# Gated mix of two long convolutions: B's results multiplied by u on the way out of PSUM, mix summing in TensorE, a new fixed order

## The chip, the cores and the metric

One core of a Trainium2 chip runs the whole kernel. The metric is the time of one execution in microseconds (us) on the device; of several executions the median counts. The engines are TensorE (PE in the profile, with its weight loads as PEld), VectorE (DVE), ScalarE (ACT), GpSimd (POOL) and SyncE (SP, which here only issues DMAs). PSUM is the memory that TensorE writes its results to, SBUF the working memory.

## The reference

Two sequence convolutions over 2048 positions and 448 channels, both with the same input u, are mixed by a gate:

```
x = A_u
g = sigmoid((x * gate_w).sum(-1, keepdims=True))
a = A(x)      # S4: x convolved with K[d,l] = Re sum_n C B dt exp(dt A l), N = 256 modes, plus x * Dskip
b = B(x)      # H3: kv = shift(k) * v; y = kv convolved with ssm_k, plus kv * ssm_D; b = x * y
out = g * a + (1 - g) * b
```

So B's convolution y is multiplied by x, element by element, before it is mixed. All inputs and the output are bf16. Written with a - b, the mix is out = b + g * (a - b), and this is how the kernel computes it.

## The kernel before

**Layout.** The 448 channels are handled as 4 groups g of 112, which lie beside one another on the partitions; each group's 112 are cut into four quarters H of NC = 28. All work runs quarter by quarter. `natu` holds u and `natv` holds kv, later B's results, each as 128 partitions x 64 x 112; `ug[H]` is the window of one quarter in `natv`, `uu` is u in `natu`. A quarter of either is 128x1792.

**Stages.** `PLAN` (line 37) gives the order in which they are written down: T0 B0 T1 b1 a0 T2 b2 a1 T3 b3 a2 m0 m1 m2 A3. T is `table(H)` (1032), which makes S4's kernel K for a quarter: exponentials and sines on ACT, products into the tiles TP and TQ on DVE, some sums by DMA with an add, and then TensorE. B and b are `conv_B(H)`, A and a are `conv_A(H)` (1055), m is `mix(H)` (1071). A convolution is a two-stage transform of both operands by matrices on TensorE (`spread`, then `transform`, 407), whose results DVE or ACT copies out of PSUM; `swapped` (803) exchanges the two halves of the partitions of one operand in eight DMAs; `products` (478) multiplies on DVE, 128x3584 twice; then come the two stages back, `stage_a` (438) and stage B. Stage B multiplies with the weights G. A b and an a that follow one another share it: `stage_b_both` (448) computes sixteen rows of B's quarter and of A's quarter in one PSUM room. In the same room TensorE subtracts B's finished results from A's with the weights `minus` (a negative identity matrix), so the room holds y of the one and a - b of another quarter's.

**What is done with the results.** For A, `epilogue_A` multiplies by the gate on the way out of PSUM (`gated`, 973) and writes over u in `natu`, since that quarter's u is no longer needed. For B, `epilogue_B` (948) copies PSUM into `ug[H]`, and after the last part of a quarter DVE multiplies the whole quarter by u. `mix(H)` adds `ug[H]` (b) and the window of `natu` (g * (a - b)) on DVE and carries the sum to the output's layout with `relay` (965): for each of the four groups four matmuls with 32 columns of `minus` each, which run side by side in the four column groups of TensorE. Their result has the wrong sign, and the copy out of PSUM (`evac.minus`) turns it. The last quarter, A3, goes through `end` (980) instead, which does the same in four parts.

**Who does what, and when.** Nothing of this is left to a scheduler. Four strings fix it, and each is indexed by the running number of a call: `SLOTS` says which of eight SBUF buffers a stage takes (the tiles q of the profile), `ROOMS` which of four PSUM rooms (the tiles ps), each 2 x 512 f32 per partition, `SIDES` which engine does each copy out of PSUM and each small scaling (S is ScalarE, V is VectorE), and for each half-tile swap which queue issues it (V is GpSimd's, S is SyncE's). All instructions are recorded as calls, and `ORDER` lists their numbers; `issue` of the class `Order` (133) issues them in this order and ties each to the one before it on its engine. So an engine runs its instructions strictly in the written order, and an instruction that waits holds up all behind it on its engine. Since every call goes through the same line of `issue`, all instructions carry line 145 in the profile; what tells them apart is tile, shape and time.

**Setup.** `Modes.run` (718) takes S4's coefficients from PSUM into the tiles hold. `hold` is a list of three tiles of one, one and two quarters; for each there are two copies for each of two coefficients.

Of the kernel before, what the change touches and what calls it, by code (L numbers as in the profile page):

```python
# [10 lines left out]
ALU = mybir.AluOpType  # L11
# [13 lines left out]
NC = 112 // NQG  # L25
# [6 lines left out]
HALVES = 1  # L32
Q_ROWS = {0: 0, 256: 1, 4: 2, 260: 3, 2: 4, 512: 5, 6: 6, 768: 7, 1024: 8, 1280: 9, 1536: 10,
# [5 lines left out]
    "60254113451327565066707216435622473722641555230367571061240"  # L39
)  # L40
ROOMS = (
    "303201320132221133023000100332000020101102013331223132233010132231223133020313021221212111021000320232120101311331120231"
    "31230230312202203230211002013123100022133320222302200321202302202333012331301212103331312131332201202032310"
)
SIDES = (
    "SSSSVVSVVVVSVVSVVVVVVVVVSVVVSSVVVSSSSSVSVVSSVVSVVSVSSVVSVVVVVVVSSSSSSSSSSSSSSSSSVVVSVSSSVSSSSSSSSSSSSSSSSVSSSSVSVSSSSSSS"
    "SSSSSSSSSSSSSVSSVSSSSSSSSSSVSSSSSSSSSSSSSSSSSSVVSVSSSSSSSSSSSSSSSSSVVVVVVVVVSVVSVVVSSSSSSVSSSSSSSSSSSSVVSVSSSSSSSSSSVSVV"
    "SSSSSSSSSSSVSSSVVSSSSSSSSSSSVSSSSVVVVVVVVSVVVVSVVVSSSVSVVSSSSSSSSSSVVVSVVSSSSSSSSSSSSSSVSSSSSVSSSSSSVSSVSVSSVSSSSVSVVSSS"
    "VSSSSVSSVVVVSSSSSSSSSSVVVSSSSVSSSSVSSSVVSS"
)  # L50
ORDER = (
# [520 lines left out]
class Part:  # L572
# [71 lines left out]
    def tables(self, H, E):  # L644
# [20 lines left out]
        add(TQ, 4, 25, 2, 2)  # L665
        q(15, 2, 2, -2, 256)
# [78 lines left out]
def body(  # L745
# [381 lines left out]
```

## Time and profile before

| | |
|---|---|
| median of three runs | 249.86 us (248.34 to 250.38) |
| the profiled execution, its own time | 247.59 us |
| its span, from first to last instruction | 245.7 us |
| mean granted clock of TensorE | 0.984 of full speed |

| stretch of the span | PE busy | DVE busy | ACT busy |
|---|---|---|---|
| 0 to 60 us | 41.1 | 57.3 | 52.4 |
| 60 to 203 us | 133.5 | 139.2 | 142.1 |
| 203 to 237 us | 33.4 | 32.7 | 23.9 |
| 237 to 245.7 us | 1.3 | 2.2 | 0.5 |

A busy time is the sum of an engine's instruction durations, with the overlap of neighbours taken out. PE's ends are modelled, so a PE that is busy all the time may still have room. A group of instructions in the profile reads: line, engine, operation, written tile <- read tiles, shapes and types, number; then busy time in us, the mean duration of one in ns; then the idle time of the engine just before them and what ended it. The chain of waits is the way back from the last instruction, at each step to what released it. The profile is that of one execution, so terms of a sum that come from it are to be set beside 247.59, not beside the median.

### The profile page before, as it was taken

To read this page: it belongs to the slowest core of one execution; us is meant where nothing else is said; L and a number is where in the kernel's file an instruction comes from. 1 tells how busy PE (TensorE), PEld (TensorE's weight loads), DVE (VectorE), ACT (ScalarE), POOL (GpSimd) and SP (SyncE) were. 2 spreads that over 40 slices of the span, in tenths; PEclk is the share of its full clock that TensorE was granted. 3 is DMA by queue.
4 is the path that set the end of the run, shared out by engine and by line. 5 is a ranking of instruction groups with operands and counts; after the bars stand their busy time and mean duration, and the time that the engine had idled before them with its cause. 6 is when DMAs were issued, how large, how long until landed. Compare 5 with 4: busy or idle time off the path is not lost.

```text
span 245.7 us, 12199 instructions
## 1 busy us (share of the span) xinstructions
PE 209.4 (85%) x5451; PEld 185.2 (75%) x5451; DVE 231.3 (94%) x399; ACT 219.0 (89%) x335; POOL 37.5 (15%) x109
## 2 busy tenths in 40 slices
PE   1557688888989999888999977999999999999970
PEld 1445256766979899788998866889999998998850
DVE  6999999999888999999999999999999999999980
ACT  3897999989999999999999999999999998657820
POOL 8600003040000014000002320000134220300000
PEclk9999799999999999999999999999999999999996
DMA  6999599999002189300476593000248720230046
GB/s 140 311 191 147 123 190 229 188 204 167 7 5 64 39 197 205 93 4 5 78 114 122 104 226 100 7 3 5 39 80 152 187 80 5 63 95 3 3 105 197
DMA packets 43443, 26.27 MB, mean 107 GB/s; under 512 B 34144, under 2 KB 40400, under 8 KB 43392
## 3 DMA queue, kind: packets, MB, share of 16 engines
q1 hardware_dynamic: 39088, 15.98, 30.6%
q0 software_dynamic: 3456, 8.60, 17.6%
q10 hardware_dynamic: 848, 0.92, 1.3%
q8 instruction: 42, 0.69, 1.1%
q14 instruction: 9, 0.07, 0.1%
HBM read 9.78 MB, written 2.87 MB: 51 GB/s over the span
## 4 chain that ended last, share of the span: by engine, by line
DVE 34%; ACT 32%; PE 21%; issue 6%; DMA 5%; DVEq 0%; ACTq 0%
PE ps L145 21%; ACT q L145 21%; DVE TQ L145 10%; DVE TP L145 9%; DVE q L145 6%; ACT G L145 4%; DVE natv L145 3%; DMA TP<-TP 2%; ACT ET L145 2%; ACT s_W L145 1%; DMA RK<-in_A_log_dt_dram 1%; DVE RK L145 1%; ACT RK L145 1%; DMA out_dram<-q 1%; DVE ET L145 1%
## 5 line engine op out<-in xcount | busy, mean ns | idle before, releaser
L145 ACT CAST q<-ps 128x896 bf16<-128x896 f32 (+3 forms) x168 | 131.6, 909 | 6.6 <-PE ps L145 6.4
L145 PEld LDWEIGHTS <-G 128*128 128x128 bf16 (+2 forms) x1136 | 35.5, 103 | 15.0 <-issue 6.0
L145 DVE TENSOR_TENSOR TQ<-TQ,ET 128x896 bf16<-128x896 bf16 (+2 forms) x70 | 45.9, 683 | 0.1
L145 PEld LDWEIGHTS <-q 128*128 128x128 bf16 (+2 forms) x784 | 41.0, 134 | 6.3 <-issue 3.5
L145 PE MATMUL ps<-q,s_W 128*128 128x112 bf16 (+1 forms) x544 | 32.6, 210 | 4.5 <-ACT q L145 2.3
L145 PE MATMUL ps<-TP,TQ 128*32 128x32 bf16 x1792 | 32.7, 240 | 2.8 <-DVE TQ L145 1.7
L145 PE MATMUL ps<-sa_R,q 128*128 128x128 bf16 x448 | 33.0, 229 | 1.5 <-issue 1.0
L145 DVE TENSOR_TENSOR q<-q,q 128x3584 bf16<-128x3584 bf16 (+1 forms) x22 | 32.3, 1510 | 1.2 <-ACT q L145 0.9
L145 PEld LDWEIGHTS <-s_W 128*128 128x128 bf16 x544 | 27.6, 97 | 7.6 <-issue 5.5
L145 PEld LDWEIGHTS <-TQ 128*32 128x32 bf16 x1792 | 29.6, 153 | 4.9 <-DVE TQ L145 1.9
L145 DVE TENSOR_TENSOR TP<-TP,ET 128x1792 bf16<-128x1792 bf16 (+3 forms) x25 | 31.7, 1270 | 0.6 <-DMA TP<-TP 0.5
L145 ACT ACTIVATE q<-hold 128x224 bf16<-128x224 f32 (+1 forms) x77 | 28.8, 461 | 0.4 <-DVE hold L145 0.3
L145 POOL DMA_DIRECT2D TP<-TP x15 | 13.4, 958 | 102.3 <-DVE TP L145 33.5
L145 POOL DMA_DIRECT2D q<-q x27 | 15.8, 638 | 57.5 <-DVE q L145 24.4
L145 PEld LDWEIGHTS <-natu 128*64 128x64 bf16 (+1 forms) x288 | 21.0, 208 | 4.6 <-DMA natu<-in_B_k_dram 3.1
L145 PE MATMUL ps<-q,G 128*128 128x56 bf16 (+1 forms) x640 | 20.3, 182 | 0.2 <-ACT q L145 0.2
L145 ACT ACTIVATE ET<-q 128x1344 bf16<-128x1344 int16 (+1 forms) x12 | 17.2, 1456 | 1.1 <-DVE TQ L145 1.0
L145 PE MATMUL ps<-Wc,natu 128*64 128x128 bf16 x224 | 16.0, 285 | 0.2 <-ACT q L145 0.2
L145 PE MATMUL ps<-Wc,natv 128*64 128x128 bf16 x224 | 15.2, 283 | 0.4
L145 PEld LDWEIGHTS <-natv 128*64 128x64 bf16 x224 | 14.7, 212 | 1.1 <-issue 0.2
L145 DVE TENSOR_TENSOR TQ<-TQ 128x448 bf16<-128x448 bf16 (+2 forms) x35 | 15.3, 443 | 0.1
L145 PE MATMUL ps<-G 112*32 112x336 bf16 (+3 forms) x448 | 13.8, 274 | 1.3 <-DVE natv L145 1.1
(97 smaller groups left out, 289.6 us busy)
## 6 DMA issues: line engine op xcount, KB each, us to landing
q<-q SPq DMA_DIRECT2D x37, 112.0 KB, 3.7
TP<-TP POOLq DMA_DIRECT2D x9, 448.0 KB, 5.8
q<-q POOLq DMA_DIRECT2D x27, 112.0 KB, 3.9
natu<-in_B_k_dram SPq DMA_DIRECT2D x2, 896.0 KB, 7.2
natv<-in_B_v_dram SPq DMA_DIRECT2D x8, 224.0 KB, 4.7
q<-in_B_ssm_k_dram SPq DMA_DIRECT2D x16, 112.0 KB, 3.9
natu<-in_A_u_dram SPq DMA_DIRECT2D x8, 224.0 KB, 5.8
TP<-TP POOLq DMA_DIRECT2D x6, 224.0 KB, 4.0
```

Source lines behind the costliest of these rows:

```text
L145: ins = f(*args, **kw)
```

## The change

1. `epilogue_B` no longer copies. DVE reads B's results from PSUM, multiplies them by u and writes b into `ug[H]`, part by part: twelve instructions of 128x448 and two of 128x896. The fourteen copies (twelve on ACT, two on DVE) and the four multiplies of a whole quarter are gone.
2. `mix` has no add. Each relay is two matmuls into the same place of PSUM, the first with b, the second with g * (a - b), which accumulate: 96 where there were 48.
3. `Modes.run` takes both halves of a tile of one quarter out of PSUM in one copy: four copies of 128x224 in place of eight of 128x112.
4. `SLOTS`, `ROOMS`, `SIDES` and `ORDER` are new throughout. By the count of the instructions, DVE has 387 where it had 399 and ACT 337 where it had 335; ten of the 64 half-tile swaps move from SyncE's queue to GpSimd's (27 to 37).
5. A function `splits` and a tuple `LATE` are added. `LATE` is empty for every quarter, so none of it is issued.

```diff
+LATE = ((), (), (), ())
...
 SLOTS = (
-    "60254113451327565066707216435622473722641555230367571061240"
+    "73475502153230513610646232057112416355041222567603341505721"
 )
 ROOMS = (
...
 SIDES = (
...
 ORDER = (
...
+    def splits(self, dst, base, src, n, step, e):
...
-            q(25, 0, 2, 2, 2)
+        late = LATE[H]
+        if 4 in late:
+            self.splits((4, 6), 25, 0, 2, 2, 2)
+        else:
+            q(25, 0, 2, 2, 2)
...
             for h0, h1, t in self.hold:
+                src = pt[:, :, 0:448].rearrange("p f (g h w) -> p f g h w", g=4, w=NC)
+                if h1 - h0 == 1:
+                    evac(t[:, 0, c].rearrange("p (f g w) -> p f g w", f=2, w=NC), src[:, :, :, h0])
+                    continue
                 for f in range(2):
-                    evac(t[:, :, c].rearrange("p h (q w) -> p q h w", w=NC)[:, 4 * f:4 * f + 4],
-                         pt[:, f, 0:448].rearrange("p (g h w) -> p g h w", g=4, w=NC)[:, :, h0:h1])
+                    evac(t[:, :, c].rearrange("p h (q w) -> p q h w", w=NC)[:, 4 * f:4 * f + 4], src[:, f, :, h0:h1])
...
     def epilogue_B(H):
         def consume(b0, n, pt):
-            evac(banked(ug[H][:, b0:b0 + n], pt), pt)
-            if b0 + n == 64:
-                V.tensor_tensor(out=ug[H], in0=ug[H], in1=window(uu, 0, 64, H), op=ALU.mult)
+            V.tensor_tensor(out=banked(ug[H][:, b0:b0 + n], pt), in0=pt, in1=banked(window(uu, b0, n, H), pt), op=ALU.mult)
         return consume
...
     def mix(H):
-        o, x = ug[H], window(uu, 0, 64, H)
-        V.tensor_tensor(out=o, in0=o, in1=x, op=ALU.add)
+        a, b = window(uu, 0, 64, H), ug[H]
         for g0 in (0, 2):
             pt = places.room()
             for i in range(2):
-                relay(pt[:, i, 0:448], g0 + i, lambda x: o[:, 16 * x:16 * x + 16], True, True)
+                for j, t in enumerate((b, a)):
+                    relay(pt[:, i, 0:448], g0 + i, lambda x: t[:, 16 * x:16 * x + 16], j == 0, j == 1)
```

More of the change, by code (lines that the diff above doesn't have):

```diff
@@ L621, in add @@
                                      in0=half(0), in1=half(1), op=ALU.add)
+    def splits(self, dst, base, src, n, step, e):
+        m, T = self.m, self.TQ
+        r = self.ET[:, ENTRY[e], 1]
+        part = list(r.ap[0])
+        for i0 in range(0, n, n if dst[-1] - dst[0] == n - 1 else 1):
+            k = n if dst[-1] - dst[0] == n - 1 else 1
+            o, s = T[:, dst[i0]], T[:, src + i0 * step]
+            self.nc.vector.tensor_tensor(
+                out=bass.AP(o.tensor, o.offset, [list(o.ap[0]), [2 * m, k], [m, 2], [(base + i0 - dst[i0]) * 2 * m, 2], [1, m]]),
+                in0=bass.AP(s.tensor, s.offset, [list(s.ap[0]), [step * 2 * m, k], [0, 2], [m, 2], [1, m]]),
+                in1=bass.AP(r.tensor, r.offset, [part, [0, k], [-m, 2], [m, 2], [1, m]]), op=ALU.mult)
+        d = T[:, dst[0]]
+        to = bass.AP(d.tensor, d.offset, [list(d.ap[0]), [2 * m * (dst[-1] - dst[0]) // max(n - 1, 1), n], [1, 2 * m]])
+        self.nc.gpsimd.dma_start(out=to, in_=T[:, base:base + n].rearrange("p n c m -> p n (c m)"), accum_op=ALU.add)
     def pairs(self, base, src, n, step, e):
@@ L671, in tables @@
         add(TQ, 7, 27, 2, -2)
-        q(27, 5, 2, 2, 512)
-        self.back(8, 16)
-        add(TQ, 8, 27, 2)
+        if 8 in late:
+            self.splits((8, 9), 27, 5, 2, 2, 512)
+            self.back(8, 16)
+        else:
+            q(27, 5, 2, 2, 512)
+            self.back(8, 16)
+            add(TQ, 8, 27, 2)
         self.back(0, 8, E[:, 8:16])
-        q(29, 8, 1, 1, 512)
+        if 10 in late:
+            self.splits((10,), 29, 8, 1, 1, 512)
+        else:
+            q(29, 8, 1, 1, 512)
         pairs(27, 9, 1, 1, 512)
-        add(TQ, 10, 29, 1)
+        if 10 not in late:
+            add(TQ, 10, 29, 1)
         pairs(11, 6, 2, -2, 256)
```

15 lines of the change are left out of this document (8 added, 7 removed), and 119 rows, old and new, of the table ORDER.

## The prediction

> **What bounds the kernel now.** I read the page's totals first, then busy time by stretch, then the chain that ended last, and only then the groups of instructions that the change touches.
>
> ```profile
> span 245.7 us, 12199 instructions
> ...
> PE 209.4 (85%) x5451; PEld 185.2 (75%) x5451; DVE 231.3 (94%) x399; ACT 219.0 (89%) x335; POOL 37.5 (15%) x109
> ...
> DVE 34%; ACT 32%; PE 21%; issue 6%; DMA 5%; DVEq 0%; ACTq 0%
> ```
>
> DVE is idle for 14.4 us of the span (245.7 - 231.3), ACT for 26.7. The chain is shared between three engines, so no share says what an edit is worth; that is a matter of where its work stands. The table by stretch (columns: stretch, its length, then busy us and count of PE, PEld, DVE, ACT, POOL):
>
> ```profile
> 150.00:185.00 35.00, 33.22 (x946) 30.75 (x948) 34.46 (x67) 34.88 (x59) 4.99 (x8) 1.00 0.17 31
> 185.00:203.00 18.00, 17.60 (x530) 16.55 (x529) 17.79 (x42) 17.25 (x24) 5.04 (x10) 1.00 0.60 137
> 203.00:215.00 12.00, 11.53 (x395) 10.73 (x392) 11.96 (x10) 9.20 (x15) 2.05 (x4) 1.00 0.16 35
> 215.00:227.00 12.00, 11.86 (x301) 10.74 (x296) 11.13 (x18) 8.09 (x15) 0.00 (x0) 1.00 0.16 49
> 227.00:237.00 10.00, 10.00 (x245) 8.17 (x246) 9.59 (x18) 6.63 (x11) 0.00 (x0) 1.00 0.02 4
> ```
>
> Up to 203 us DVE and ACT are full together. From 203 on ACT has slack (23.9 us of work in the 34 us to 237), while DVE (32.7) and PE (33.4) are full. So this is a kernel with two full engines in its body and another pair in its tail. The chain of waits through the tail (start, length, what):
>
> ```profile
> 203.03 3.37 DVE q L145 x2
> ...
> 208.03 3.96 DVE q L145 x2
> 211.99 2.00 DVE natv L145 x2
> 213.99 0.61 DVE q L145
> ...
> 214.65 12.17 PE ps L145 x305
> ...
> 226.96 9.17 PE ps L145 x210
> ```
>
> The two pairs of "DVE q" are the products of b3 and a2. Behind them stand two instructions on natv, which are the very ones the change removes; then PE runs to the end. In the order of time DVE reads:
>
> ```profile
> 211.90 2.09 DVE L145 TENSOR_TENSOR natv<-natv,natu 128x1792 bf16<-128x1792 bf16 x2
> ...
> 214.51 1.08 DVE L145 TENSOR_TENSOR natv<-natv,natu 128x1792 bf16<-128x1792 bf16 x1
> ...
> 225.33 1.69 DVE L145 TENSOR_TENSOR q<-q,q 128x896 bf16<-128x896 bf16 x3
> ...
> 229.18 2.10 DVE L145 TENSOR_TENSOR natv<-natv,natu 128x1792 bf16<-128x1792 bf16 x2
> ```
>
> Five of the seven natv instructions lie behind 211 us, none of them beside an idle DVE.
>
> **The change part by part.** The groups, by shape (busy us, mean ns of one, then idle time before):
>
> ```profile
> L145 ACT CAST q<-ps 128x512 bf16<-128x512 f32 x43 | 26.4, 637 | 3.3 <-PE ps L145 3.1
> ...
> L145 DVE TENSOR_TENSOR natv<-ps,natv 128x896 bf16<-128x896 f32 x8 | 8.5, 1081 | 0.0
> ...
> L145 DVE TENSOR_TENSOR natv<-natv,natu 128x1792 bf16<-128x1792 bf16 x7 | 7.4, 1085 | 0.0
> ...
> L145 DVE TENSOR_TENSOR natu<-ps,gt 128x448 bf16<-128x448 f32 x12 | 7.3, 617 | 0.0
> ...
> L145 DVE TENSOR_SCALAR q<-hold 128x224 int32<-128x224 f32 x26 | 6.6, 299 | 0.0
> ...
> L145 ACT ACT_TABLE_LOAD x5 | 6.4, 1283 | 1.3 <-PEq L1111 1.2
> L145 ACT CAST natv<-ps 128x448 bf16<-128x448 f32 x10 | 6.4, 639 | 1.2 <-PE ps L145 1.1
> ...
> L145 DVE CAST q<-ps 128x512 bf16<-128x512 f32 x9 | 5.9, 685 | 0.1
> ...
> L145 ACT ACTIVATE q<-hold 128x224 int32<-128x224 f32 x13 | 4.9, 421 | 0.0
> ...
> L145 PE MATMUL ps<-natv,minus 128*32 128x448 bf16 x48 | 3.0, 355 | 0.0
> ...
> L145 ACT CAST natv<-ps 128x896 bf16<-128x896 f32 x2 | 2.3, 1128 | 0.0
> ...
> L145 DVE CAST natv<-ps 128x448 bf16<-128x448 f32 x2 | 1.2, 616 | 0.0
> ```
>
> I price by busy time over count, since neighbours overlap a little.
>
> B's results: the seven natv instructions go (four multiplies by u, three adds of mix), 7.4 us of DVE. The evictions of B go: 8.7 us of ACT and 1.2 of DVE. In their place DVE reads PSUM and multiplies: twelve of 128x448, which no row shows, but which differ from the twelve gated ones (7.3 us) only in the second operand, and two of 128x896, like natv<-ps,natv (2 x 1.06 = 2.1). By itself this gives DVE -7.4 - 1.2 + 7.3 + 2.1 = +0.8, and ACT -8.7: the multiply alone makes DVE no lighter.
>
> The new deal of evictions (SIDES) spends what ACT won. Counted in both programs' instructions, ACT takes five casts of 128x512 from DVE (DVE -3.3, ACT +3.1) and six int32 phases (-1.5, +2.3); smaller kinds make some -2.0 on DVE and +3.3 on ACT, an estimate from their rows. One more table load stands on ACT, +1.28. In sum DVE gets -6.8 from this and ACT +10.0. Altogether DVE loses 6.0 us (231.3 to 225.3) and ACT gains 1.3 (219.0 to 220.3).
>
> The table load is at ACT's head, before the exponential of log_dt, where ACT waits:
>
> ```profile
> 4.22 0.21 ACT L145 ACTIVATE TP<-RK 112x4 bf16<-112x4 bf16 x1 [1.74 <-DMA RK<-in_A_log_dt_dram]
> ```
>
> 1.28 fits into 1.74, so I cost it at nothing; without that cover it is 1.28. The Trainium skill, "ScalarE: Activation LUTs", section "What ACT_TABLE_LOAD costs", budgets about 2.7 us for each switch of table set. By the page the load would outlast that wait by about 1 us; by the row, which decides here, it does not.
>
> mix: three adds of 1.06 go from DVE (counted above); PE gets 48 more matmuls. The 48 of today take 3.0 us, four column groups side by side, so 48 more take at most 3.0, at least 0 where PE stands anyway.
>
> Setup loses four small copies out of PSUM, some 0.6 us of DVE, counted in the deal above.
>
> Now the path. Upstream of the products of a2, ACT's work in the new order is about 4 us more than before (its share of a2's transform is eight evictions, not seven; b3's end 2.3 us of work later), DVE's 2 us less. The table load hides, so ACT comes about 2.6 us late at a2. What cover had it?
>
> ```profile
> 200.73 3.38 ACT L145 CAST q<-ps 128x896 bf16<-128x896 f32 x4
> ```
>
> The second and third of these four are a2's last on ACT, so they are done near 203.3, while the products start at 208.03, behind DVE's own cast and b3's products. A2's data are then there at 205.9, b3's near 202.6, and DVE does b3 from 202.6 to 206.6 and a2 to 210.5: 1.5 us before 212.0.
>
> From there on DVE's list to the last product of A3 is 13.1 us against 15.0 (225.33 + 1.69 - 212.0), priced by the same rows: the natv pair is not there, and four multiplies of 0.61 are. That gives 223.6 where it was 227.0, 3.4 earlier. PE, released by the cast behind the natv pair (213.99), could begin 3.5 earlier too. But 40 of the 48 added matmuls stand in this stretch of its queue, 40 x 63 ns = 2.5 us, ahead of a2's stage B, and everything of A3 is queued behind them. In the row 215 to 227 PE is busy for 11.86 of 12 by a modelled end, with 301 matmuls, 39 ns each. Its groups tell more:
>
> ```profile
> 217.18 0.58 PE L145 MATMUL ps<-q,s_W 128*128 128x56 bf16 x16
> ...
> 220.44 1.40 PE L145 MATMUL ps<-q,s_W 128*128 128x56 bf16 x48
> ```
>
> 32 more cost 0.82, 26 ns each: a group of 16 is 0.41 of issue and 0.17 of run-out. So some of PE's busy time takes further work, and I put a third of the 2.5 on the path, 0.8 (both ends: 0 and 2.5). The other 8 matmuls are in the last stretch, +0.5. The sum: -3.4 + 0.8 + 0.5 = -2.1, and the lighter DVE behind 227 (two natv instructions less among its 9.59 of 10) gives perhaps 0.3 more: **-2.4 us**, span 243.3. With the 1.9 us that lie around the span the profiled execution was 247.59 and would be 245.2. The median of the three runs shown is 249.86, 2.27 above that execution; so the median to expect is **247.5**. With none of the relays hidden and none of the 0.3 it is -0.4; with all hidden and ACT as early as before, -5.
>
> Ten of the 64 half-tile swaps move from SP's queue to POOL's (27 to 37).
>
> ```profile
> q<-q SPq DMA_DIRECT2D x37, 112.0 KB, 3.7
> ...
> q<-q POOLq DMA_DIRECT2D x27, 112.0 KB, 3.9
> ```
>
> ```profile
> L145 DVE TENSOR_TENSOR q<-q,q 128x3584 bf16<-128x3584 bf16 x14 | 27.8, 2019 | 1.2 <-ACT q L145 0.9 <-issue 0.2
> ```
>
> 0.2 us each, and the idle time ahead of the products names ACT, not a DMA (the row of 128x3584): nothing. What they pass in POOL's queue are the additive copies of TP, and the swaps that now stand ahead of those read operands that are written earlier than the copies' sources.
>
> **The rivals.**
>
> PE gives it all back (0.15). If PE in the tail has no room at all, the 3.0 us stand on the path, against 3.4: -0.5 to +1.0, so 249.4 to 250.9. For it speaks 10.00 of 10.
>
> The whole DVE relief arrives (0.18): the order was laid anew, DVE idles no longer than its 14.4, and the span falls by 6.0 to 239.7, median 243.9. Against it speaks that ACT, with 220.3, would have to idle 7 us less than now.
>
> Slower: DVE keeps PSUM rooms (0.17). A room of the joint stage B was emptied by DVE and ACT side by side (617 and 639 ns); now by DVE alone, one after the other, so it comes free 0.6 us later, and with four rooms in all PE waits for it. In the tail that is four rooms of a2, 4 x 0.6 = 2.4, with the relays' 3.0 unhidden, against at most 2.0 of the natv pair; and ACT's 1.3 more, uncovered, in the body. Together +4.7 (2.4 + 3.0 - 2.0 + 1.3): 254.6. It decides once DVE's queue between the two reads of a room holds other work, as A3's products of 0.6 do in the new order. Against it: DVE has 4.7 us less to do there.
>
> The swaps on POOL come late (0.05): three stages whose queue changed most (B0, b1, a0) each wait for a swap held up until a DVE instruction of 2.0 us ends, up to 6 - 2.4 = +3.6, 253.5. The Trainium skill, "SBUF — State Buffer", section "Who interferes with whom", has such a lock between VectorE and a queue of GpSimd; the 0.2 us between the two rows above speaks for little of it.
>
> **How the numbers follow.** The forecast, with its own range of -0.4 to -5 (245 to 249.5), has 0.45. The three runs shown span 0.8%, so 1% is what can be told from no change: 247.4 and 252.4 are the edges. Faster by over 1%: all of the full relief (0.18) and 0.25 from the forecast, whose centre lies at that edge, 0.43. Slower: 0.17 and 0.03 of the swaps' 0.05, 0.20. Within: the rest, 0.37. The range takes in the full relief down to 1.0 under its centre, half of what the three runs shown span, and above it reaches nearly the centre of the slower case: 242.9 to 254.0, leaving out about half of that case and some of the relief.
>
> **What would show it.** DVE busy near 225, ACT near 220, six table loads with no idle time behind the first two. In the tail no natv pair between the products of a2 and PE's run; the products of a2 done near 210.5; 96 relays in near 6.0 us busy. Wrong if DVE's idle time rises by over 6 us, if DVE's products wait for ACT or a DMA for more than 2 us in sum, or if PE's waits for DVE's reads of ps show up in the tail.

## The result: slower by 1.3%, and the profile after

The kernel after took 252.49 us (median of four runs, 252.19 to 252.90) beside 249.41 of the kernel before (four runs, 248.34 to 250.38): a ratio of 1.0126, 95% interval 1.0078 to 1.0173. A second measurement (after_again, below) gave 1.0157 (1.0120 to 1.0193). The forecast was a gain of 1%; the time lies inside the range and on the other side of no change.

The profiled execution of after took 252.9 us, 0.4 above its median. That of before, 247.59, was the fastest execution seen of that kernel, 1.8 below its median. So the two spans (251.1 and 245.7) differ by 5.4 us where the medians differ by 3.1, and a part of what lies between the two traces is the difference of two executions, not of two kernels. The page of after (span, busy time, shares of the chain):

```profile
span 251.1 us, 12289 instructions
...
PE 211.7 (84%) x5499; PEld 187.2 (75%) x5499; DVE 225.7 (90%) x387; ACT 221.6 (88%) x337; POOL 43.8 (17%) x119
...
ACT 47%; PE 25%; DVE 14%; issue 6%; DMA 5%; SPq 0%; ACTq 0%; DVEq 0%
```

DVE lost 5.6 us of work, as priced (225.7; forecast 225.3), and its idle time rose from 14.4 to 25.4 us (251.1 - 225.7). The work went and the time didn't. Where DVE's new idle time lies, the table by stretch tells (length, then busy us and count of PE, PEld, DVE, ACT, POOL):

```profile
185.00:203.00 18.00, 17.57 (x492) 16.26 (x491) 17.83 (x42) 16.84 (x24) 6.96 (x13) 1.00 0.72 157
203.00:215.00 12.00, 10.97 (x383) 10.17 (x378) 11.14 (x12) 8.79 (x13) 0.52 (x1) 1.00 0.23 61
215.00:227.00 12.00, 11.71 (x291) 10.09 (x289) 6.36 (x8) 9.00 (x18) 0.00 (x0) 1.00 0.01 3
227.00:237.00 10.00, 10.00 (x240) 8.76 (x232) 7.81 (x15) 6.48 (x10) 0.00 (x0) 1.00 0.02 4
```

From 185 to 203 us DVE has 17.83 of 18, as before (17.79). From 215 to 227 it has 6.36 us of work where it had 11.13, while PE is as full as before (11.71 against 11.86). The groups that the change touches, by shape:

```profile
L145 DVE TENSOR_TENSOR natv<-ps,natu 128x448 bf16<-128x448 f32 x12 | 7.4, 616 | 0.6 <-PE ps L145 0.5
...
L145 PE MATMUL ps<-natv,minus 128*32 128x448 bf16 x48 | 4.4, 356 | 0.0
L145 PE MATMUL ps<-natu,minus 128*32 128x448 bf16 x48 | 4.4, 352 | 0.0
...
L145 ACT ACT_TABLE_LOAD x6 | 7.7, 1283 | 1.3 <-PEq L1140 1.2
```

The multiply out of PSUM takes 616 ns, like the gated one that it was priced by (617). The order of time on DVE, from the products of a2 (start, length, instruction, number; in brackets the idle time ahead and who ended it):

```profile
211.45 2.02 DVE L145 TENSOR_TENSOR q<-q,q 128x3584 bf16<-128x3584 bf16 x1
213.39 0.75 DVE L145 CAST q<-ps 128x256 bf16<-128x256 f32 x2
215.12 0.62 DVE L145 CAST RK<-ps 128x448 bf16<-128x448 f32 x1 [0.98 <-PE ps L145]
216.90 2.69 DVE L145 CAST q<-ps 128x512 bf16<-128x512 f32 x3 [1.16 <-PE ps L145]
220.38 0.96 DVE L145 CAST q<-ps 128x768 bf16<-128x768 f32 x1 [0.79 <-PE ps L145]
224.88 1.09 DVE L145 CAST q<-ps 128x896 bf16<-128x896 f32 x1 [3.54 <-PE ps L145]
226.00 1.70 DVE L145 TENSOR_TENSOR q<-q,q 128x896 bf16<-128x896 bf16 x3
...
232.72 0.62 DVE L145 TENSOR_TENSOR q<-q,q 128x896 bf16<-128x896 bf16 x1
```

Four times DVE waits for a PSUM tile that PE has yet to write: 0.98 + 1.16 + 0.79 + 3.54 = 6.5 us between the products of a2 and the first product of A3. In the trace of before the first such product starts at 220.07, and DVE doesn't wait once on the way there from 212.0:

```profile
217.37 2.78 DVE L145 CAST q<-ps 128x512 bf16<-128x512 f32 x4
220.07 0.62 DVE L145 TENSOR_TENSOR q<-q,q 128x896 bf16<-128x896 bf16 x1
```

The same shows in the waits of the tail, from 203 us to the end (engine and what it waits for: us in total, times, the longest). After:

```profile
ACT q L145 <- PE ps L145: 10.6, 6, 3.1
DVE q L145 <- PE ps L145: 7.5, 4, 3.5
```

Before:

```profile
ACT q L145 <- PE ps L145: 7.3, 12, 1.4
...
DVE q L145 <- PE ps L145: 0.6, 1, 0.6
```

PE is what they wait for, and the chain of waits says the same: from 207.80 us on it is PE up to 243 us, with 24.26 us in its last piece.

```profile
207.80 4.07 PE ps L145 x166
...
218.74 24.26 PE ps L145 x598
```

To compare all kernels alike I took a few points of time out of each trace. The first column is the end of the last product of a2, from the start of the span; the others count from there, in us: start of A3's first product on DVE, end of A3's last product there, end of the last relay on PE, end of the last copy out of PSUM, end of the span.

| kernel | a2 done | A3 first | A3 last | last relay | last copy | end |
|---|---|---|---|---|---|---|
| before | 212.0 | 8.1 | 15.0 | 28.2 | 28.8 | 33.7 |
| after | 213.5 | 12.5 | 19.9 | 31.0 | 31.8 | 37.6 |
| after, second measurement | 213.1 | 12.3 | 19.7 | 30.8 | 31.6 | 37.8 |

So the tail is 3.9 us longer, more than the 3.1 by which the medians differ: 4.4 are lost up to the first product of A3 and 0.4 up to the last, 2.0 are won back from there to the last relay, and 1.1 lost behind it, 0.9 of them after the last copy.

The 4.4 us fall into two parts. A3's first transform group on PE, which feeds its products, starts 7.8 us behind a2 (221.28 - 213.47), where it started 5.2 behind it (217.18 - 211.99): 2.6 us. From that group to the first product it takes 4.7 us, where it took 2.9: 1.8 us. In before the first product in DVE's list needs the first group alone; in after it needs the third, which starts at 224.21.

```profile
219.81 0.97 PE L145 MATMUL ps<-WcK,RK 128*64 128x128 bf16 x28
...
221.28 0.58 PE L145 MATMUL ps<-q,s_W 128*128 128x56 bf16 x16
...
224.21 0.58 PE L145 MATMUL ps<-q,s_W 128*128 128x56 bf16 x16
```

Of the traces of the experiments below, the five that have the order of before all through (mult_alone, mix_alone, merge_alone, all_but_order, mult_b1) show 2.9 us for the second part, like before; those in the order of after, and its variants, all show 4.7.

That the body is 1.5 us later here is chance at least in part: single executions of three kernels below that differ from before only in the setup or behind that point have 212.8, 212.8 and 213.7.

### The profile page after: what moved, and what is told of

Its sections match the earlier page's. It is cut to its first block, busy times and chain, and to the rows that moved or that the text cites. A ratio compares the mean times of both kernels' runs of the same rounds, so it can differ in the third digit from the quotient of the medians.

```text
span 251.1 us, 12289 instructions
## 1 busy us (share of the span) xinstructions
PE 211.7 (84%) x5499; PEld 187.2 (75%) x5499; DVE 225.7 (90%) x387; ACT 221.6 (88%) x337; POOL 43.8 (17%) x119
## 4 chain that ended last, share of the span: by engine, by line
ACT 47%; PE 25%; DVE 14%; issue 6%; DMA 5%; SPq 0%; ACTq 0%; DVEq 0%
ACT q L145 35%; PE ps L145 25%; ACT G L145 4%; DVE TP L145 4%; ACT ET L145 3%; DMA natu<-in_A_u_dram 3%; ACT RK L145 2%; DVE q L145 2%; DVE natv L145 2%; DVE TQ L145 2%; DMA RK<-in_A_log_dt_dram 2%; DVE ET L145 1%; ACT s_W L145 1%; ACT L145 1%; DVE G L145 1%
## 5 line engine op out<-in xcount | busy, mean ns | idle before, releaser
L145 ACT CAST q<-ps 128x896 bf16<-128x896 f32 (+3 forms) x171 | 131.2, 899 | 12.5 <-PE ps L145 10.3
L145 PE MATMUL ps<-q,s_W 128*128 128x112 bf16 (+1 forms) x544 | 33.4, 210 | 5.7 <-ACT q L145 4.5
L145 PE MATMUL ps<-TP,TQ 128*32 128x32 bf16 x1792 | 33.5, 241 | 4.2 <-issue 3.4
L145 PE MATMUL ps<-sa_R,q 128*128 128x128 bf16 x448 | 33.6, 229 | 2.3 <-issue 1.9
L145 PEld LDWEIGHTS <-TQ 128*32 128x32 bf16 x1792 | 30.4, 153 | 6.6 <-issue 4.6
L145 DVE TENSOR_TENSOR TP<-TP,ET 128x1792 bf16<-128x1792 bf16 (+3 forms) x25 | 31.6, 1271 | 0.0
L145 ACT ACTIVATE q<-hold 128x224 bf16<-128x224 f32 (+1 forms) x83 | 30.9, 429 | 0.1
L145 POOL DMA_DIRECT2D q<-q x37 | 21.8, 630 | 37.7 <-ACT q L145 34.0
L145 PE MATMUL ps<-Wc,natv 128*64 128x128 bf16 x224 | 16.2, 297 | 2.1 <-DVE natv L145 2.1
L145 PE MATMUL ps<-Wc,natu 128*64 128x128 bf16 x224 | 15.3, 284 | 0.0
L145 DVE CAST q<-ps 128x256 bf16<-128x256 f32 (+4 forms) x13 | 9.4, 748 | 6.5 <-PE ps L145 5.8
```

The lines of the kernel that those rows point to most:

```text
L145: ins = f(*args, **kw)
```

## The experiments

All times are medians, all ratios are against the kernel before on the same chip, with the 95% interval. Twelve of the eighteen ratios lie outside every range that was written down ahead of them, three of these by less than 0.1% (mix_alone, no_second, no_sums). In kernels made from the kernel before, `nc.skip()` records an empty call, `nc.joined` hangs an instruction on the call ahead of it, and `evac.vector()` uses up the copy's letter in SIDES, so that the numbers in ORDER keep their meaning. `LEFT_OUT` holds numbers that are not issued, `FORCED` sets the engine of one copy.

**The parts alone, in the old order.** First the multiply alone (`mult_alone`), then mix alone (`mix_alone`), then the merged copies of setup alone (`merge_alone`), then all three with the old order (`all_but_order`).

```diff
 # mult_alone
-            evac(banked(ug[H][:, b0:b0 + n], pt), pt)
+            evac.vector()
+            V.tensor_tensor(out=banked(ug[H][:, b0:b0 + n], pt), in0=pt, in1=banked(window(uu, b0, n, H), pt), op=ALU.mult)
             if b0 + n == 64:
-                V.tensor_tensor(out=ug[H], in0=ug[H], in1=window(uu, 0, 64, H), op=ALU.mult)
+                nc.skip()
```

> The kernel before with the change of B's results alone: DVE multiplies by u straight from PSUM at the places where the copies stood, the four multiplies of 128x1792 and the copies (8.7 us of ACT, 1.2 of DVE) are gone; order and all else as before. Theory P: DVE has +0.8 us in sum, but in the tail one multiply of 1.06 us leaves the way of TensorE's run; ACT's relief of 8.7 us meets a DVE that is as full as before: ratio 0.994 to 1.000. Theory O: the same sign, up to 3 us of gain, 0.988 to 0.996. Rival R (PSUM rooms stay taken longer, since DVE alone empties them, 0.62 us after one another, and TensorE waits): ratio 1.004 to 1.016.

```diff
 # mix_alone
-        o, x = ug[H], window(uu, 0, 64, H)
-        V.tensor_tensor(out=o, in0=o, in1=x, op=ALU.add)
+        a, o = window(uu, 0, 64, H), ug[H]
+        nc.skip()
...
-                relay(pt[:, i, 0:448], g0 + i, lambda x: o[:, 16 * x:16 * x + 16], True, True)
+                relay(pt[:, i, 0:448], g0 + i, lambda x: o[:, 16 * x:16 * x + 16], True, False)
+                nc.joined = nc.calls[-1]
+                relay(pt[:, i, 0:448], g0 + i, lambda x: a[:, 16 * x:16 * x + 16], False, True)
+                nc.joined = None
```

> The kernel before with the change of mix alone: the three DVE adds of mix (128x1792, 1.06 us each) are gone, and behind each group of four relays stand four more with natu; order, deal, rooms and buffers are as before. Theory P (TensorE's queue bounds the tail, so each added relay stands on the path at some 0.05 us, 48 x 0.05 = 2.4 us, and of the adds only the one ahead of TensorE's long run, 1.06 us, is worth time): ratio 1.003 to 1.008 against the kernel before. Theory O (the new order loses the time, the new computation does not): the relays hide where TensorE waits anyway, ratio 0.992 to 0.998.

```diff
 # merge_alone
             for h0, h1, t in self.hold:
+                if h1 - h0 == 1:
+                    src = pt[:, :, 0:448].rearrange("p f (g h w) -> p f g h w", g=4, w=NC)
+                    evac(t[:, 0, c].rearrange("p (f g w) -> p f g w", f=2, w=NC), src[:, :, :, h0])
+                    evac.vector()
+                    nc.skip()
+                    continue
```

> The kernel before with the third change of the computation alone: four copies of 128x224 in place of eight of 128x112 in the setup, everything else and the order as before. If the setup's DVE is on the path: 0.6 us less, ratio 0.996 to 0.999. If not, 0.999 to 1.002.

The fourth has these three edits together.

> All three changes of the computation (B's multiply from PSUM, mix with two relays, the merged copies of the setup) in the order, deal, rooms and buffers of the kernel before: what is left out of the change is the new order. Theory P: the relays' 2.4 us against two DVE instructions of 1.06 us that leave the way of TensorE's run: ratio 0.996 to 1.004. Theory O: the computation gains and the new order loses, ratio 0.985 to 0.994, some 4 us or more under the changed kernel (1.0126).

| kernel | time | ratio |
|---|---|---|
| mult_alone | 256.65 | 1.0286 (1.0239 to 1.0333) |
| mix_alone | 251.51 | 1.0085 (1.0055 to 1.0115) |
| merge_alone | 250.18 | 1.0004 (0.9979 to 1.0029) |
| all_but_order | 258.40 | 1.0353 (1.0312 to 1.0394) |

The parts add up (2.9 + 0.9 + 0.0 against 3.5%). So the new computation is dear where it is put into the old order, and the new order wins 2% back. What the multiply brings shows in the waits from 97 to 203 us. In mult_alone:

```profile
ACT q L155 <- PE ps L155: 8.6, 12, 2.2
PE ps L155 <- DVE natu L155: 3.4, 6, 1.0
PE ps L155 <- DVE natv L155: 2.5, 2, 1.7
```

In before, of these:

```profile
PE ps L145 <- DVE natu L145: 0.8, 2, 0.5
```

PE waits 5.9 us for DVE to empty rooms of stage B, where it waited 0.8 us (3.4 of it in rooms that DVE reads twice, 2.5 in those of B0, which hold B alone). The wait is handed on: ACT waits 8.6 us for PE (the same line of before has 0.7). This is the loop that the rival "DVE keeps PSUM rooms" described. One of its places is on PE's timeline of mult_alone, where three groups of the next transform each stand behind a gated read by DVE:

```profile
143.80 0.55 PE L155 MATMUL ps<-q,s_W 128*128 128x112 bf16 x8 [0.89 <-DVE natu L155]
...
145.87 0.55 PE L155 MATMUL ps<-q,s_W 128*128 128x112 bf16 x8 [0.49 <-DVE natu L155]
...
148.53 0.55 PE L155 MATMUL ps<-q,s_W 128*128 128x112 bf16 x8 [1.05 <-DVE natu L155]
```

The products of a2 end at 220.0 us there, against 212.0, so most of the loss lies in the body. The waits are not all of it: up to that point DVE, the fullest engine, has 3.8 us more work (209.2 us against 205.4) and 4.2 us more idle time. The +0.8 of the forecast counted the three adds of mix as gone, and this kernel keeps them. What the waits alone cost, and what the work alone, no run parts. mix_alone is another matter. Its program is that of before up to 211 us and its tail is the same to A3's last product (15.0); the last relay ends 30.1 us behind a2, not 28.2. 1.9 us is nearly the whole price of 48 more relays at the pace that after shows (one group of four every 0.19 us: 12 x 0.19 = 2.3):

```profile
225.11 0.36 PE L145 MATMUL ps<-natv,minus 128*32 128x448 bf16 x4
225.29 0.36 PE L145 MATMUL ps<-natu,minus 128*32 128x448 bf16 x4
```

**The multiply in one quarter alone.** `mult_b1` is mult_alone with the new lines under `if H == 1`.

```diff
+            if H == 1:
+                evac.vector()
+                V.tensor_tensor(out=banked(ug[H][:, b0:b0 + n], pt), in0=pt, in1=banked(window(uu, b0, n, H), pt), op=ALU.mult)
+                if b0 + n == 64:
+                    nc.skip()
+                return
```

> The kernel before with B's results of one quarter alone, b1's, multiplied by u from PSUM (the four copies and the multiply of 128x1792 of that quarter are gone); the order and all else as before. Rival R (a room of the joint stage B is now read twice by DVE, one read behind the other and behind table work, TensorE waits for the room and ACT for TensorE): this quarter has some 4 us of the 7 us that all four cost, ratio 1.010 to 1.020, with waits of TensorE for DVE's reads of natv and natu between 135 and 150 us. If it is the load of DVE as a whole and not the rooms: 0.998 to 1.004.

It took 250.97 us, 1.0068 (1.0042 to 1.0093), and the waits from 97 to 203 us stand between those of the two others:

```profile
ACT q L155 <- PE ps L155: 4.2, 7, 1.2
...
PE ps L155 <- DVE natu L155: 2.5, 4, 1.0
```

One quarter of the four costs 0.7% of 2.9, and brings the same kind of wait: about a share that fits its number, so no single place makes the loss. Here too DVE has more to do, 232.6 us against 231.3, which is near the 1.6 us that the time rose by. In after neither line of DVE is there: from 97 us on, PE waits for no natu or natv, and ACT waits 1.7 us for PE. In the new order the loop of the rooms is gone.

**The two natv instructions behind a2.** Of the 3.4 us that the forecast put on DVE, 1.9 are its shorter list behind a2, and the going of this pair (2.0 us) is the largest term in that. `pair_late` leaves the kernel before as it is and moves them out of that place, five copies later.

```diff
 ORDER = (
-5468 5866 6026 ... 5155 4496 6027 ... 5719
+5468 6026 ... 5155 6027 ... 5719 4496 5866
```

> The kernel before with its pair of DVE instructions on natv (2.0 us, between a2's products and the copy that releases TensorE's run) moved behind the five copies out of PSUM that follow; the same instructions, the same number on each engine. The prediction's step (the pair stands on the way of TensorE's run, so without it the tail is up to 2.0 us earlier): ratio 0.992 to 0.997. If DVE's list up to A3's first products decides, in whatever order: 0.998 to 1.003.

It took 250.35 us, 1.0052 (1.0023 to 1.0081), slightly more than before. DVE in its trace, behind the products of a2:

```profile
213.28 1.08 DVE L158 TENSOR_TENSOR natv<-natv,natu 128x1792 bf16<-128x1792 bf16 x1
215.81 0.96 DVE L158 CAST q<-ps 128x768 bf16<-128x768 f32 x1 [1.45 <-PE ps L158]
...
220.75 2.09 DVE L158 TENSOR_TENSOR natv<-natv,natu 128x1792 bf16<-128x1792 bf16 x2
```

Where the pair stood DVE now waits 1.45 us for PE, and PE runs no earlier: A3's first transform group starts 5.1 us behind a2 (217.86 - 212.77), in before 5.2. The pair was on the chain of waits of before, and yet it held PE up by 0.1 us at most: it filled a wait for PE that was there anyway. That A3's first product then comes 10.0 us behind a2, not 8.1, tells nothing more, since the pair now stands right ahead of it.

**Single parts of after.** `mix_undone` goes back to one relay and the add on DVE, joined to the relay that is written first. In the new order the second half of m0's relays runs ahead of that relay, so half of m0's output carries b alone.

```diff
-                for j, t in enumerate((b, a)):
-                    relay(pt[:, i, 0:448], g0 + i, lambda x: t[:, 16 * x:16 * x + 16], j == 0, j == 1)
+                n0 = len(nc.calls)
+                relay(pt[:, i, 0:448], g0 + i, lambda x: b[:, 16 * x:16 * x + 16], True, True)
+                if g0 == i == 0:
+                    nc.joined = nc.calls[n0]
+                    V.tensor_tensor(out=b, in0=b, in1=a, op=ALU.add)
+                    nc.joined.insert(0, nc.joined.pop())
+                    nc.joined = None
+                for _ in range(4):
+                    nc.skip()
```

> The changed kernel with mix as it was: one DVE add of 128x1792 ahead of the first relay of each mix, 48 relays in place of 96, the order otherwise as changed. Theory P: 48 x 0.05 = 2.4 us leave TensorE's queue, and the adds fall into DVE's idle time of the tail (5.6 us between 215 and 227 us): ratio 1.000 to 1.005 against the kernel before, where the changed kernel has 1.0126. Theory O: TensorE's run is late for other reasons, the adds put a wait of 1.06 us in front of the relays: ratio 1.010 to 1.016.

`no_second` has one relay and no add.

```diff
-                for j, t in enumerate((b, a)):
-                    relay(pt[:, i, 0:448], g0 + i, lambda x: t[:, 16 * x:16 * x + 16], j == 0, j == 1)
+                relay(pt[:, i, 0:448], g0 + i, lambda x: b[:, 16 * x:16 * x + 16], True, True)
+                for _ in range(4):
+                    nc.skip()
```

> The changed kernel without the 48 added matmuls: each relay of mix carries b alone, so the output lacks g * (a - b) for three of the four quarters; all else as changed (ratio 1.0126 against the kernel before). Theory P (the tail is bound by TensorE's queue, so 48 x 0.05 us = 2.4 us come off the end): ratio 1.001 to 1.005. Theory V (the tail is bound by DVE's queue: A3's last products, which the end needs, stand behind B's multiplies; the relays only delay A3's last transform group by 24 matmuls, 1.2 us): ratio 1.006 to 1.010. If the relays hide: 1.011 to 1.014.

`b3_on_act` gives the last quarter of B its copies and its multiply back.

```diff
+            if H == 3:
+                nc.scalar.copy(banked(ug[H][:, b0:b0 + n], pt), pt)
+                if b0 == 32:
+                    nc.joined = nc.calls[-1]
+                    V.tensor_tensor(out=ug[H], in0=ug[H], in1=window(uu, 0, 64, H), op=ALU.mult)
+                    nc.joined = None
+                return
```

> The changed kernel with B's results of the last quarter alone handled as before: four copies by ACT where DVE's multiplies stood, and one DVE multiply of 128x1792 behind the last copy (behind A3's last product in DVE's queue). Theory V: three multiplies of 0.62 us leave the way of A3's last product, 1.85 us: ratio 1.003 to 1.008. Theory P: DVE is not what the tail waits for: ratio 1.010 to 1.015.

`no_ahead` leaves out the 48 relays that stand ahead of the last stage B, `no_sums` the last 64 sums of T3 on PE, and `no_both` both.

```diff
+LEFT_OUT = {*range(5894, 5910), *range(5876, 5892), *range(5912, 5928)}  # no_ahead
+LEFT_OUT = {*range(5052, 5116)}  # no_sums
...
-            for group in self.calls[int(a):int(b or a) + 1]:
-                for f, args, kw in group:
+            for at, group in enumerate(self.calls[int(a):int(b or a) + 1], int(a)):
+                for f, args, kw in () if at in LEFT_OUT else group:
```

> The changed kernel without the 48 relays that stand ahead of the last stage B (all of m1's, half of m0's, both operands; their copies out of PSUM stay, so that part of the output is not computed). Theory P (TensorE's work between a2's products and A3's transform and stage B sets the tail: 48 x 0.052 = 2.5 us): stage B starts 2.5 us earlier after a2's products, ratio 1.003 to 1.007 against the kernel before. Theory W (the engines hand the four PSUM rooms round, and TensorE's lighter queue only becomes waits for ACT and DVE, as where 24 of these 48 were left out and nothing was gained): 1.010 to 1.015.

> The changed kernel without the last 64 matmuls of T3's sums, which stand behind b3's stage A on TensorE (1.1 us; part of A3's table is not computed). In the kernel before they were done ahead of it. Theory P: 1.1 us, ratio 1.008 to 1.011. Theory W: 1.012 to 1.015.

> The changed kernel without either, the 48 relays ahead of the last stage B and the last 64 of T3's sums. Theory P: 3.6 us, ratio 0.998 to 1.004, and from the end of a2's products to the start of the last stage B 10.6 us, where the changed kernel has 14.2 and the kernel before 9.8. Theory W: 1.009 to 1.014.

`after_again` is after with no edit, as the measure for these.

> The changed kernel once more, with more runs, beside the same runs of the kernel before: 1.010 to 1.016. Theory W expects it no more than 0.4% above no_ahead (1.0116) and no_second (1.0143) and 0.4 to 0.9% above no_sums (1.0073).

| kernel | time | ratio | a2 done | A3 first | A3 last | last relay | end |
|---|---|---|---|---|---|---|---|
| after_again | 252.93 | 1.0157 (1.0120 to 1.0193) | 213.1 | 12.3 | 19.7 | 30.8 | 37.8 |
| mix_undone | 252.38 | 1.0113 (1.0070 to 1.0156) | 212.2 | 12.3 | 19.5 | 30.9 | 37.5 |
| no_second | 252.97 | 1.0143 (1.0107 to 1.0179) | 214.3 | 12.6 | 19.8 | 29.7 | 36.6 |
| b3_on_act | 253.14 | 1.0150 (1.0109 to 1.0191) | 211.5 | 12.0 | 18.4 | 31.5 | 38.0 |
| no_ahead | 252.38 | 1.0116 (1.0081 to 1.0152) | 214.1 | 12.6 | 19.8 | 30.6 | 37.7 |
| no_sums | 251.36 | 1.0073 (1.0046 to 1.0099) | 213.2 | 11.7 | 19.0 | 30.2 | 36.8 |
| no_both | 251.85 | 1.0096 (1.0061 to 1.0131) | 213.8 | 11.8 | 19.0 | 29.8 | 36.9 |

mix costs nothing that can be told in the new order: with no second relay at all, or with the 48 ahead of the last stage B gone, the time stays within the interval of after (1.0078 to 1.0173). The trace of no_second has a tail 1.2 us shorter, behind A3, and a body as much longer; its median shows neither. Taking the 48 away brings nothing forward: no_ahead has A3's first product at 12.6 and its last at 19.8, like after. The T3 sums seem to cost something. no_sums is the only one whose interval lies apart from that of after_again, though not from that of the first measurement of after, and no_both, which lacks the same sums, has 1.0096. In their traces A3's first product comes 0.7 and 0.5 us earlier behind a2 than in after_again, and the end 1.0 and 0.8; PE spends 1.20 us on the sums in after:

```profile
213.87 1.20 PE L145 MATMUL ps<-TP,TQ 128*32 128x32 bf16 x64
```

The wait behind them is as long without them (DVE of no_sums): the whole list has merely come earlier.

```profile
223.72 1.09 DVE L156 CAST q<-ps 128x896 bf16<-128x896 f32 x1 [3.54 <-PE ps L156]
```

b3_on_act brings A3's last product 1.3 us forward, as the B multiplies among A3's products are gone, but a multiply of the whole quarter comes later, behind a wait for ACT, and the end gains nothing:

```profile
229.26 0.61 DVE L155 TENSOR_TENSOR q<-q,q 128x896 bf16<-128x896 bf16 x1
232.44 1.09 DVE L155 TENSOR_TENSOR natv<-natv,natu 128x1792 bf16<-128x1792 bf16 x1 [2.56 <-ACT natv L155]
```

**Mending the order.** Five kernels reorder after by hand. `relays_late` moves the 48 relays of no_ahead, with their six copies, behind A3's stage A.

```diff
-5685 5894-5909 5702 6171 5876-5891 5703 5910 6175 6087-6102 5911 6105 5912-5927 6103 ... 6192
+5685 5702 6171 5703 6175 6087-6102 6105 6103 ... 6192 5894-5909 5910 5911 5876-5891 5892 5893 5912-5927 5928 5929
```

> The changed kernel with 48 of the 96 relays (and their six copies out of PSUM) moved from ahead of the last stage B to behind A3's stage A in the order; the same instructions. Theory P, if the place of the relays decides (stage B starts 2.5 us earlier): ratio 1.002 to 1.007. If TensorE's total after the products decides, wherever the relays stand: 1.010 to 1.014. Theory V: A3's last transform group comes 1.6 us earlier (32 relays of 0.05 us are ahead of it), some of it given back at the end: 1.006 to 1.011.

`stores` does the copy of the end's last part on ACT (one letter of SIDES is changed for it) and puts it with its four stores ahead of m2's last copy, so that these store the last rows of that part before m2 has written them all.

```diff
-5965 6352 6425 6353-6368 6426 6369 6373 6428 6427 6372 6371 6429 6370
+6425-6429 5965 6352-6369 6373 6372 6371 6370
```

> The changed kernel with the copy out of PSUM of the last but one part of A3's end on ACT, ahead of m2's last copy, and its four stores ahead of those of the last part. In the changed kernel four stores stand behind one another in ACT's queue after the last copy (1.75 us), in the kernel before two (0.86 us). If this is a part of the loss: 0.9 us less, ratio 1.007 to 1.010. If the last landing does not hang on it: 1.011 to 1.014.

`t3_first` puts the last T3 sums ahead of b3's stage A, their copy on ACT, and A3's last transform group ahead of 16 of the relays.

```diff
-5116-5147 5498-5505 5444-5459 5649 5462-5477 5460 5052-5115 5506 5478 5507 5479 4856-4871 5461 5148 5480-5495 5149-5205 ...
+5116-5147 5052-5115 5498-5505 5444-5459 5649 5148 5462-5477 5460 5461 5149-5205 5506 5478 5507 5206 5479 4856-4871 5480-5495 ...
-5894-5909 5702 6171 5876-5891 5703 5910 6175 6087-6102 5911 6105 5912-5927 6103
+5894-5909 5702 6171 6087-6102 5703 6103 6175 5876-5891 5910 6105 5911 5912-5927
+FORCED = {5148: 'S'}
```

> The changed kernel with another order in the tail: the last 64 matmuls of T3's sums ahead of b3's stage A on TensorE (they stood behind it), their copy out of PSUM on ACT (DVE did it behind the products), T3's last gather right behind, and A3's last transform group ahead of 16 of the 32 relays before it. Theory T (the tail is late because A3's second half of the table comes out of TensorE's queue late: from the end of a2's products to A3's first product 12.5 us, 8.1 in the kernel before): A3's first product 2 to 4 us earlier, ratio 1.002 to 1.008 against 1.0126 to 1.015 as changed. If the tail is bound by the sum of TensorE's work behind the products, wherever it stands: 1.011 to 1.015.

`ends` takes m2's last copy, and the last copy but one with its stores behind it, forward.

```diff
-5964 6374-6406 ... 6351 6259 6258 5965 6352 6425 6353-6368 6426 6369 6373 6428 6427 6372 6371 6429 6370
+5964 5965 6374-6406 ... 6351 6425-6429 6259 6258 6352 6353-6368 6369 6373 6372 6371 6370
+FORCED = {6425: 'S'}
```

> The changed kernel with m2's last copy out of PSUM ahead of A3's last but one parts on ACT, and the copy of the last but one part on ACT with its four stores right behind it, so that only the last part's four stores are left after the last copy, as in the kernel before. If the four stores in one queue (1.75 us behind the last copy, 0.86 in the kernel before) are a part of the loss: 0.9 us, ratio 1.008 to 1.011. If not: 1.012 to 1.015.

`t3_ends` has the edits of the last two.

> Both orders, t3_first and ends, in one kernel. Theory T and the stores together: ratio 0.998 to 1.005; each part without effect: 1.011 to 1.015.

| kernel | time | ratio |
|---|---|---|
| relays_late | 254.52 | 1.0216 (1.0172 to 1.0259) |
| stores | 255.13 | 1.0241 (1.0200 to 1.0282) |
| t3_first | 256.07 | 1.0289 (1.0244 to 1.0335) |
| ends | 253.71 | 1.0166 (1.0126 to 1.0207) |
| t3_ends | 257.64 | 1.0322 (1.0276 to 1.0368) |

None of them helps, and t3_first, which was to bring A3 forward, puts its first product at 15.1 us behind a2 in place of 12.5. DVE's waits there are longer, not shorter:

```profile
216.49 1.22 DVE L159 CAST q<-ps 128x1024 bf16<-128x1024 f32 x1 [3.08 <-PE ps L159]
...
226.57 1.09 DVE L159 CAST q<-ps 128x896 bf16<-128x896 f32 x1 [3.54 <-PE ps L159]
```

In this kernel PE waits twice for ACT between 216 and 220 us, for 0.91 and 1.01 us, where in after it waits for no other engine from a2 to these stages' end: with b3's stage A and the gather moved, the copies on ACT end too late for what is now next on PE. The sums came earlier and what depends on them did not. A3's first transform group starts 10.4 us behind a2 there (222.97 - 212.60); from it to the first product it is 4.7, as in after. No version that was run beats the kernel before. The end of after stays dear as well: the last stores on ACT's queue of after

```profile
245.33 1.75 ACTq L145 DMA_DIRECT2D out_dram<-q  x4
```

and of before

```profile
240.81 0.86 ACTq L145 DMA_DIRECT2D out_dram<-q  x2
```

are four against two, 0.44 us each, which fits the 0.9 us behind the last copy. That was not tried by itself: in stores and ends more was moved, and in ends one store on each of the two queues took 1.31 us.

## Why the prediction was wrong

**DVE's work: right.** -6.0 us was forecast, -5.6 came. The instruction prices held, and so did six table loads: 1283 ns each, and the added one is hidden at ACT's head, where the exponential still waits for the DMA, 0.39 us now where it was 1.74:

```profile
2.94 1.28 ACT L145 ACT_TABLE_LOAD   x1
4.61 0.20 ACT L145 ACTIVATE TP<-RK 112x4 bf16<-112x4 bf16 x1 [0.39 <-DMA RK<-in_A_log_dt_dram]
```

By the 2.7 us that the Trainium skill ("ScalarE: Activation LUTs", section "What ACT_TABLE_LOAD costs") budgets it would have shown. That budget is a load of about 1283 ns, with which these rows agree, and a drain of about 1380 ns, which the trace of after doesn't show: in its body one load stands between an activation that ends at 109.47 us and one that starts at 110.78, 1.31 us for the whole switch. The measured figure decides.

**ACT's work: the sign right, the size off.** +1.3 was forecast, +2.6 came (221.6). The +10.0 of the new deal was short by 1.3; its smaller kinds were an estimate.

**The swaps: right.** The rival of the lock between VectorE and GpSimd's queue left no sign. The median time to landing on GpSimd's queue in after is the last number of

```profile
q<-q POOLq DMA_DIRECT2D x37, 112.0 KB, 4.0
```

4.0 us on the queue that took ten more, 3.9 before; and the idle time of DVE's products is 1.4 us in the whole of after, for ACT.

**a2 done at 210.5: wrong.** It was 213.5 (213.1 in the second measurement). The step said that DVE has 2 us less ahead of it and that ACT's extra work is covered. ACT's last cast for a2, however, ends at 209.4 where it ended at 203.3: ACT had 6.6 us more work up to there, not some 4, so the cover of 4.7 us that the prediction counted (203.3 to 208.03) was used up. ACT is not what made a2 late, though: DVE does the four products of b3 and a2 from 205.65 on without a wait. It is late itself. Up to a2's end it has 1.2 us less work, not 2, and its idle time rose from 6.6 to 9.3 us where the prediction added none; 1.5 of these 2.7 us lie between 60 and 80 us (rows in the last section).

**The step that failed: "From there on DVE's list to the last product of A3 is 13.1 us against 15.0".** The list was right, 13.2 us by the trace. That it sets the time was wrong: it took 19.9 us, with 6.7 us of waits in it, 6.5 of them for PE. So where the forecast won 1.9 us behind a2, which with the 1.5 ahead of it made its term of -3.4, the trace loses 4.8. The forecast's own sign, DVE's idle time up by over 6 us, came as well (11.0). The prediction read it off the chain of waits of before, in which the natv pair stands between two pieces of other engines, and from DVE's 11.13 of 12. Both are true and neither says that PE had room behind DVE. PE was as full (11.86 of 12) and the sentence beside it, that some of PE's busy time takes further work, was applied to the relays and not to the path. pair_late shows the other half: with the pair gone from its place in before, DVE waits there, and PE's first transform group for A3 starts no earlier (5.1 us behind a2, 5.2 in before). What the runs showed in the place of DVE's list is PE's queue: from a2 to A3's first product PE is idle for 0.3 us in all in after.

**The relays, a third of 2.5 us on the path: too much here, too little elsewhere.** In after the second relays cost nothing that can be told in the medians (no_second, mix_undone, no_ahead), and at most the 1.2 us by which no_second's tail is shorter; in the old order the change of mix costs 0.85%, near their whole price. The term of 0.8 us was not what failed. The forecast for their busy time, near 6.0 us, is 8.8 as the page counts it (4.4 twice), but the two groups run into each other: by their starts 96 take 24 x 0.19 = 4.6 us.

**The rivals.** "DVE keeps PSUM rooms" named a mechanism that the new computation does bring: in the old order it is a part of the 2.9% of mult_alone, beside DVE's added work. It had it in the wrong place, the tail, and in the new order it is gone. So the time fell on that rival's side for another reason; that it lies inside the range, which reaches up to this rival, is luck. "PE gives it all back" is the nearest to what came, though the time lies above its 250.9: PE was what the tail waited for, with the difference that its price is not the relays. "The whole DVE relief arrives" fell with DVE's idle time: its condition was that this stays at 14.4 us, and it is 25.4.

**What the 3.9 us are.** Shown: they lie between a2 and the first product of A3, and at the very end. Of the 4.4 us up to the first product, 2.6 stand ahead of A3's first transform group. The last T3 sums, which PE had done by 211.79 in before and does at 213.87 in after, are 0.5 to 0.7 of these by no_sums and no_both. Fitting, not tried: the spread of A3's second half (0.97 us at 219.81) is now ahead of that group, too, where in before it came behind it. The other 1.8 are the same in every trace of the new order, and an argument from the trace of after, not tried, says why: the cast of 224.88 waits 3.54 us, and two products of A3 whose operands were out of PSUM at 223.3 stand behind it in DVE's written order. Fitting as well, not tried alone: two more stores at the end, 0.9. So what lengthens the tail up to the first product is the new order and not the new computation: all_but_order, which has that computation in the old order, has its first product 7.9 us behind a2. Which of the order's moves make most of the loss stays open.

## What to carry to other kernels

An instruction that stands on the chain of waits need not be worth its length: look at what the engine waits for if it goes, and whether the engine that feeds it has room in the same stretch. Where two reads of one PSUM room move from two engines to one, look for the price on TensorE and on whoever waits for it, too, and not only on the engine that got the work. When an engine's idle time rises by as much as the work taken from it, or by more (11.0 and 5.6 us here), the work was taken where the engine was not the bound.

## What the runs showed of the hardware

TensorE's granted clock differs between executions of the same program. mix_alone has the program of before up to 211 us, and its first products end 1.0 us later (77.75 and 76.74), those of a2 1.8 us later (213.75 and 211.99). The rows from 60 to 80 us, of before and of mix_alone (behind the five engines: granted clock, share of DMA, GB/s):

```profile
60.00:80.00 20.00, 19.33 (x640) 17.97 (x641) 17.62 (x21) 20.00 (x31) 0.52 (x1) 1.00 0.13 31
```

```profile
60.00:80.00 20.00, 18.54 (x621) 17.30 (x621) 16.59 (x19) 19.11 (x29) 0.52 (x1) 0.91 0.09 19
```

and of after:

```profile
60.00:80.00 20.00, 16.67 (x582) 15.40 (x584) 16.15 (x20) 18.95 (x32) 5.46 (x9) 0.84 0.52 92
```

In the traces of the new order this stretch has 0.76 to 0.91; in those of the old order it has 1.00 in all but two, which have 0.91. Whether the low clock delays PE there, or a PE that waits more is granted less, these runs don't tell; and pair_late, with 1.00 there, has a2 0.8 us later than before all the same. It may be a part of why the body gained nothing. From 203 to 237 us both kernels have 1.00.
